# Retention and a gated FFN on one core: four products and six table instructions moved from GpSimd to VectorE, four zero products removed

## The chip, the cores and the metric

The kernel runs on one NeuronCore of a Trainium2 chip. A core has five engines, each with its own instruction queue in program order: TensorE (PE; its weight loads are listed as PEld) multiplies matrices, VectorE (DVE) and ScalarE (ACT) work on tiles, GpSimd (POOL) works on tiles and also issues transfers, and SyncE (SP) issues transfers. Sixteen DMA engines move the data. The metric is the device time of one execution in microseconds (us). Lower is better.

## The reference

For every batch and head a 64 x 64 state runs over 768 tokens, and its output feeds a gated FFN:

```python
# q, k, v: (B=4, H=8, S=768, D=64), float32
for t in range(S):
    state = gamma[h] * state + outer(k[:, :, t], v[:, :, t])
    y[:, :, t] = 1 / sqrt(D) * (q[:, :, t] @ state)
x = y.transpose(0, 2, 1, 3).reshape(3072, 512)
out = (sigmoid(x @ w_gate) * (x @ w_val)) @ w_out      # d_ff = 1536
```

with gamma[h] = 1 - 2^(-5-h).

## The kernel before, in words

The recurrence is done in blocks of 128 tokens (C). Within a block, scores k x q are multiplied by a decay table and then with v; between blocks, a state is summed from scaled k and v. A step `i` stands for one token block and two of the four batches (`t, h = divmod(i, 2)`), so there are twelve. All four batches of one token block, 512 rows, make one FFN tile `t`; there are six. The FFN of a tile has twelve column groups of 128 for gate and value (`up`), each followed by a sigmoid on ACT (line 419) and a product on DVE (line 420), and then the product with `w_out` (`down`).

The schedule is by hand: the order of the calls in the program is the order on each engine. There is no planner with costs. Lines 470 to 501 do the first tile's retention (steps 0 and 1) on a path of its own: transposes on PE (`first_transpose`), scores, products with v (`first_y`). `keep_on(n)` (line 461) puts n products of a zero tile on PE between them; nothing reads their results. Lines 510 to 531 are the first tile's gate and value groups. After this, lines 542 to 574 do the first tile's `down` together with step 2, whose k and q are transposed on PE (`transpose`, line 209). From step 3 on k and q are transposed by DMA (`xbar`, line 216, issued on SP), and the table `plan` (line 577) says after which FFN group each retention block comes.

All loads except two come from POOL's queue (`nc.gpsimd.dma_start`): they convert float32 to bf16 on the way. The order on that queue is: the first tile's k, q and v (line 95), weights of gate and value in slices of 256 columns (line 82, slices 0 to 5), `w_out` in four parts (line 89), and k, q and v of the later steps (lines 66, 70, 60). From `load_next(4)` on, a one-element copy on POOL (`hold`, line 539) waits for a transposed tile before further loads are issued. Every load on POOL after the first eight waits on one of eight semaphores, in turn: so an issue waits until the load eight before it has landed.

Three sets of POOL instructions that are no loads stand between these issues ahead of step 2. `first_scaled` (line 369) makes the scaled k of steps 0 and 1, the tiles `ks`, in four products of 128 x 512; `first_state` (line 372) needs them. `later_tables` (line 176) makes `tabsk` in four copies of 128 x 24 and `maskk` in two products of 128 x 512; `scale_k` (line 222, on POOL) and `mask` (line 251, on DVE) read them from step 2 on.

PE's results go to eight PSUM banks in rotation (`bank`, line 200): each new tile waits until the readers of the one eight before it are done.

Of the kernel before, what the change touches and what calls it, by code (L numbers as in the profile page):

```python
# [11 lines left out]
ALU = mybir.AluOpType  # L12
# [3 lines left out]
def kernel(  # L16
# [12 lines left out]
    nc = tc.nc  # L29
    B, H, S, D = q.shape  # L30
    N_TOK, D_MODEL = out.shape
    D_FF = moe_w_gate.shape[1]
    C = 128
    NT = S // C
    NP = H // 2
# [14 lines left out]
    kn, qn, ks, vs, kqT = {}, {}, {}, {}, {}  # L50
# [29 lines left out]
    def load_w(dst, w, s, kk=slice(0, KT)):  # L80
        cols = slice(s * 256, (s + 1) * 256)
        nc.gpsimd.dma_start(out=dst[:, kk, cols], in_=w.rearrange("(kk p) n -> p kk n", p=128)[:, kk, cols])  # L82

    def load_gate_val(s):
        load_w(wg, moe_w_gate, s)
        load_w(wv, moe_w_val, s)
# [17 lines left out]
    def entry(t, j):  # L104
        return t[:, j * H:(j + 1) * H, :]
# [25 lines left out]
    causal = const.tile([128, 128], F32, name="causal")  # L131
    decay = const.tile([128, 2, NP, C], F32, name="decay")
    maskk = const.tile([128, 2, NP, C], F32, name="maskk")
    tabs = const.tile([128, H, NT], F32, name="tabs")
# [20 lines left out]
    def exps_y(p):  # L155
        nc.scalar.activation(taby[:, p], col, AX.Exp, bias=lsc, scale=lgz[:, 0, p:p + 1])
# [19 lines left out]
    def later_tables():  # L176
        src = tabs.rearrange("s (p e) t -> s e t p", e=2)
        dst = tabsk.rearrange("s t j (p e) -> s j e t p", e=2)
        for j in range(2):
            for e in range(2):  # L180
                nc.gpsimd.tensor_copy(dst[:, j, e], src[:, e ^ j])
        for e in range(2):
            nc.gpsimd.tensor_tensor(maskk[:, e], causal.unsqueeze(1).to_broadcast([128, NP, C]),
                                    tabsk[:, 0, e, 0::2].unsqueeze(2).to_broadcast([128, NP, C]), op=ALU.mult)


# [13 lines left out]
    def bank(shape, dt=F32):  # L200
        return pf.tile(shape, dt, tag="ff", name="ff")
# [4 lines left out]
    def new_kqT(i):  # L206
        kqT[i] = at.tile([128, 2, 2, NP, C], BF16, tag="kqT", name="kqT", bufs=2)
# [142 lines left out]
    def first_scores(i, j):  # L350
        scores(i, j)
        for e, st in enumerate((stA, stB)):
            st[i, j] = at.tile([128, NP, C], BF16, tag=f"sf{e}", name=f"sf{e}", bufs=4)
            nc.vector.tensor_tensor(st[i, j], sc[i, j][e], decay[:, e], op=ALU.mult)

    def first_y(i, j, engs):
        if 0 not in xT:
            new_xT(0, 2)
        c = (2 * i + j) * C
        n = 1 if engs[0] is engs[1] else 2  # L360
        os = [bank([128, NP // n, C]) for _ in range(n)]
        for p in range(NP):
            for e, st in enumerate((stA, stB)):
                nc.tensor.matmul(os[p * n // NP][half(e), p % (NP // n), :], vs[i][:, j * H + 2 * p + e, :], st[i, j][:, p, :],
                                 start=(p % (NP // n) == 0), stop=True, skip_group_check=True)
        for g, eng in enumerate(engs):
            eng(xT[0][g][:, :, c:c + C], os[g] if n == 2 else os[0][:, 2 * g:2 * g + 2])

    def first_scaled(i, j, x):
        nc.gpsimd.tensor_tensor(entry(ks[i], j), x, tabs[:, :, 0].unsqueeze(2).to_broadcast([C, H, D]), op=ALU.mult)  # L370

    def first_state(i):
        z = bank([128, 2, NP, D])
# [87 lines left out]
    def keep_on(n):  # L461
        u = bank([128, 512])
        for _ in range(n):
            nc.tensor.matmul(u, zero[:, :128], zero, start=True, stop=True)  # L464
# [4 lines left out]

    new_kqT(0)  # L470
    new_kqT(1)
    keep_on(11)
    exps_y(0)
    first_transpose(0, 0, 0, dve)
    first_transpose(0, 0, 1, act)
# [5 lines left out]
    exps_y(1)  # L481
    first_transpose(1, 0, 0, act)
    exps_y(2)
    keep_on(1)
    first_scores(0, 1)
    first_transpose(1, 0, 1, act)
    keep_on(2)
# [5 lines left out]
    keep_on(2)  # L493
    first_y(0, 0, (act, act))
    first_scores(1, 1)
    keep_on(1)
    first_y(0, 1, (act, act))
    keep_on(2)
    first_y(1, 0, (dve, act))
# [1 line left out]
    first_y(1, 1, (dve, act))  # L501
    nc.scalar.preload_act_table(AX.Sigmoid)
    first_scaled(0, 0, kf)
    first_scaled(0, 1, entry(kn[0], 1))
    load_gate_val(3)
    first_scaled(1, 0, entry(kn[1], 0))
    first_scaled(1, 1, entry(kn[1], 1))
    load_gate_val(4)
    load_gate_val(5)
    for n1s in ((0, 1), (2, 3)):  # L510
        gates = first_parts(wg, n1s, (3 * C,) if n1s[0] == 0 else ())
        for n1, *ps in zip(n1s, gates, first_parts(wv, n1s)):
# [1 line left out]
    last_constants()  # L514
    zero_scores()
    later_tables()
    gates = [up_part(0, wg, (n1,)) for n1 in (4, 5)]
    for n1, gate in zip((4, 5), gates):
# [111 lines left out]
```

## Time and profile before

| | |
|---|---|
| median of 11 runs | 226.13 us (225.66 to 227.27) |
| the profiled execution | 226.52 us, its span 224.8 us |
| PE busy | 217.0 us, 97% of the span |
| DVE / ACT / POOL busy | 123.0 / 70.6 / 106.8 us |
| mean of DMA engines' busy share | 90% or more in the first 20 of 40 slices |
| first FFN product on PE | 14.90 us |
| last FFN product ends, first tile's transposes of step 2 begin | 37.9 us |
| products of zeros on PE | 19, the first at 1.20 us |

Times in the profile count from the start of the span. The span is 1.7 us shorter than the time of its own execution. A group's busy time is the sum of its instructions; where an engine was idle, the profile names what released it. For a load, "to landing" is the time from its issue on the queue until its last byte is there.

### The profile page before, as it was taken

Reading aid. Unit: us, or ns where it says so; the run is one execution under the profiler, and the core shown is the slowest. Engines: PE = TensorE matmul, PEld = TensorE weight load, DVE = VectorE, ACT = ScalarE, POOL = GpSimd, SP = SyncE. Lnnn points to the kernel's source line nnn. Section 1 sums busy time; section 2 is a strip of 40 time slices with the busy share of each in tenths; the row PEclk is TensorE's granted clock in tenths of the full one; section 3 lists DMA queues with packets and bytes.
Section 4 is the critical chain, followed back from the end, with each engine's and each line's share of the span. In section 5 each row is a group of like instructions: output and inputs, shape, how many; then the busy total and the mean of one; then the engine's idle time right before and its main releaser. Section 6 shows DMA issues by size and latency. Waiting matters only on the chain.

```text
span 224.8 us, 6389 instructions
## 1 busy us (share of the span) xinstructions
PE 217.0 (97%) x2765; PEld 127.1 (57%) x2770; DVE 123.0 (55%) x242; ACT 70.6 (31%) x122; POOL 106.8 (48%) x130
## 2 busy tenths in 40 slices
PE   7899998999999998999999999999999999999994
PEld 2554443459999665556556556555555555555554
DVE  6753873085894784945925754934654922333301
ACT  4883332334233211332321433321433321333221
POOL 8999997886983945909467082460000000000000
PEclk9999999999999999999999999999999999999999
DMA  9999999999999999999979979999600012100022
GB/s 130 145 173 189 160 178 168 184 152 270 133 151 131 120 139 195 157 106 61 139 107 194 163 50 114 79 137 143 140 3 0 3 47 96 47 4 0 4 93 93
DMA packets 105820, 25.84 MB, mean 115 GB/s; under 512 B 94784, under 2 KB 102848, under 8 KB 105792
## 3 DMA queue, kind: packets, MB, share of 16 engines
q0 software_dynamic: 80960, 13.90, 85.9%
q1 hardware_dynamic: 23648, 11.21, 24.1%
q8 instruction: 21, 0.34, 0.7%
q10 hardware_dynamic: 1184, 0.33, 0.6%
q14 instruction: 7, 0.06, 0.1%
HBM read 28.31 MB, written 6.29 MB: 154 GB/s over the span
## 4 chain that ended last, share of the span: by engine, by line
PE 60%; DMA 20%; POOL 18%; issue 1%; DVE 0%; POOLq 0%; SPq 0%
PE ff L391 56%; DMA kqX<-qn 7%; DMA qn<-in_q_dram 4%; DMA wo<-in_moe_w_out_dram 3%; DMA kn<-in_k_dram 3%; POOL wv L82 2%; POOL wg L82 2%; POOL ks L370 2%; DMA kqX<-kn 2%; PE ff L278 2%; POOL kn L70 2%; POOL vs L95 2%; POOL kn L66 1%; POOL kn L95 1%; POOL qn L95 1%
## 5 line engine op out<-in xcount | busy, mean ns | idle before, releaser
L420 DVE TENSOR_TENSOR hT<-gs,ff 128x512 bf16<-128x512 f32 x72 | 48.4, 686 | 51.9 <-PE ff L391 46.4
L391 PE MATMUL ff<-xT,wg 128*64 128x512 bf16 (+2 forms) x607 | 70.0, 346 | 0.1
L391 PE MATMUL ff<-xT,wv 128*64 128x512 bf16 (+2 forms) x608 | 70.0, 345 | 0.0
L419 ACT ACTIVATE gs<-ff 128x512 f32<-128x512 f32 x72 | 42.8, 597 | 82.9 <-PE ff L391 80.3
L391 PE MATMUL ff<-wo,hT 128*64 128x512 bf16 (+3 forms) x580 | 64.6, 361 | 0.1
L391 PEld LDWEIGHTS <-wv 128*64 128x64 bf16 (+1 forms) x608 | 35.4, 109 | 23.4
L391 PEld LDWEIGHTS <-hT 128*64 128x64 bf16 (+1 forms) x582 | 32.7, 109 | 27.1
L391 PEld LDWEIGHTS <-wg 128*64 128x64 bf16 (+1 forms) x608 | 34.9, 109 | 23.2 <-DVE xT L294 0.2
L261 DVE TENSOR_TENSOR st<-ff,maskk 128x256 bf16<-128x256 f32 (+2 forms) x76 | 35.1, 492 | 9.0 <-PE ff L248 8.0
L441 ACT COPY ob<-ff 128x512 f32<-128x512 f32 x23 | 13.5, 586 | 57.6 <-PE ff L391 57.5
L294 DVE TENSOR_TENSOR xT<-ff,taby 128x512 bf16<-128x512 f32 x20 | 12.9, 686 | 24.3 <-PE ff L278 24.3
L540 POOL COPY held<-kqX 128x1 bf16<-128x1 bf16 x7 | 1.3, 185 | 36.0 <-DMA kqX<-qn 33.8
L224 POOL TENSOR_TENSOR ks<-kn,tabsk 128x1024 bf16<-128x1024 bf16 x8 | 15.6, 1947 | 1.6 <-DMA kn<-in_k_dram 1.6
L70 POOL DMA_DIRECT2D qn<-in_q_dram x20 | 15.5, 803 | 0.0
L70 POOL DMA_DIRECT2D kn<-in_k_dram x20 | 15.2, 774 | 0.0
L60 POOL DMA_DIRECT2D vs<-in_v_dram x10 | 12.1, 1212 | 1.1 <-DMA wo<-in_moe_w_out_dram 0.9
L66 POOL DMA_DIRECT2D kn<-in_k_dram x10 | 9.3, 928 | 1.8 <-issue 1.7
L314 DVE TENSOR_TENSOR zb<-za,tabz 128x512 bf16<-128x512 f32 x10 | 9.4, 943 | 0.0
L66 POOL DMA_DIRECT2D qn<-in_q_dram x10 | 9.3, 925 | 0.0
L464 PE MATMUL ff<-zero 128*128 128x512 bf16 x19 | 7.6, 527 | 1.2 <-DVE zero L139 1.2
L278 PE MATMUL ff<-st,vs 128*64 128x128 bf16 x160 | 6.4, 222 | 0.0
L82 POOL DMA_DIRECT2D wg<-in_moe_w_gate_dram x8 | 6.4, 822 | 0.0
(74 smaller groups left out, 117.3 us busy)
## 6 DMA issues: line engine op xcount, KB each, us to landing
out_dram<-ob SPq DMA_DIRECT2D x23, 256.0 KB, 2.8
vs<-in_v_dram POOLq DMA_DIRECT2D x10, 256.0 KB, 7.4
kn<-in_k_dram POOLq DMA_DIRECT2D x13, 128.0 KB, 4.9
qn<-in_q_dram POOLq DMA_DIRECT2D x13, 128.0 KB, 4.9
wo<-in_moe_w_out_dram POOLq DMA_DIRECT2D x4, 384.0 KB, 7.1
kn<-in_k_dram POOLq DMA_DIRECT2D x20, 64.0 KB, 3.8
qn<-in_q_dram POOLq DMA_DIRECT2D x20, 64.0 KB, 4.5
wg<-in_moe_w_gate_dram POOLq DMA_DIRECT2D x4, 256.0 KB, 5.2
```

The lines of the kernel that those rows point to most:

```text
L60: nc.gpsimd.dma_start(out=vs[i], in_=v[2 * h:2 * h + 2, :, t * C:(t + 1) * C, :].rearrange("b h s d -> s (b h) d"))
L66: nc.gpsimd.dma_start(out=tiles[i][:, 0:H], in_=src[0])
L70: nc.gpsimd.dma_start(out=dst[:, e], in_=pairs[:, 1 - e])
L82: nc.gpsimd.dma_start(out=dst[:, kk, cols], in_=w.rearrange("(kk p) n -> p kk n", p=128)[:, kk, cols])
L224: nc.gpsimd.tensor_tensor(ks[i], kn[i], tabsk[:, i // 2].rearrange("s j h -> s (j h)").unsqueeze(2) .to_broadcast([C, 2 * H, D]), op=ALU.mult)
L261: nc.vector.tensor_tensor(st[i, j][to, :, n], sc[i, j][e][of, :, n], maskk[to, e ^ j, :, n], op=ALU.mult)
L278: nc.tensor.matmul(y[i, j][half(e), p, :], vs[i][:, j * H + 2 * p + e, :], st[:, p, :], start=False, stop=True, skip_group_check=True)
L294: nc.vector.tensor_tensor(xT[t][0][:, :, c:c + C], y[i, j], taby, op=ALU.mult)
L391: nc.tensor.matmul(o[c], w[:, c], x, **marks)
L419: nc.scalar.activation(g, ps[0], AX.Sigmoid)
L420: nc.vector.tensor_tensor(hT[t][:, n1s[0]:n1s[-1] + 1, lo:hi], g.rearrange("p (i n) -> p i n", n=n), ps[1].rearrange("p (i n) -> p i n", n ...
L441: nc.scalar.copy(ob, o)
```

## The change

The four products of `first_scaled` and the six instructions of `later_tables` go from POOL's queue to DVE's; their operands, results and place among the calls stay. On POOL the three loads of weight slices 3, 4 and 5 then follow one another. Of `keep_on`'s products, two of the first eleven go, and two single ones later.

```diff
@@ later_tables
         for j in range(2):
             for e in range(2):
-                nc.gpsimd.tensor_copy(dst[:, j, e], src[:, e ^ j])
+                nc.vector.tensor_copy(dst[:, j, e], src[:, e ^ j])
         for e in range(2):
-            nc.gpsimd.tensor_tensor(maskk[:, e], causal.unsqueeze(1).to_broadcast([128, NP, C]),
+            nc.vector.tensor_tensor(maskk[:, e], causal.unsqueeze(1).to_broadcast([128, NP, C]),
                                     tabsk[:, 0, e, 0::2].unsqueeze(2).to_broadcast([128, NP, C]), op=ALU.mult)
@@ first_scaled
     def first_scaled(i, j, x):
-        nc.gpsimd.tensor_tensor(entry(ks[i], j), x, tabs[:, :, 0].unsqueeze(2).to_broadcast([C, H, D]), op=ALU.mult)
+        nc.vector.tensor_tensor(entry(ks[i], j), x, tabs[:, :, 0].unsqueeze(2).to_broadcast([C, H, D]), op=ALU.mult)
@@ the order of the first tile
     new_kqT(0)
     new_kqT(1)
-    keep_on(11)
+    keep_on(9)
     exps_y(0)
...
     exps_y(2)
-    keep_on(1)
     first_scores(0, 1)
...
     first_scores(1, 1)
-    keep_on(1)
     first_y(0, 1, (act, act))
...
     first_scaled(0, 0, kf)
     first_scaled(0, 1, entry(kn[0], 1))
-    load_gate_val(3)
     first_scaled(1, 0, entry(kn[1], 0))
     first_scaled(1, 1, entry(kn[1], 1))
-    load_gate_val(4)
-    load_gate_val(5)
+    for n in range(3, 6):
+        load_gate_val(n)
```

## The prediction

> **What bounds the kernel now.** I read the page first, then PE's waits by stretch, then the timelines of PE, POOL and DVE, and last the rate of the transfers in quarter microseconds.
>
> The page's first part says that PE is nearly always busy, so only its 7.8 us of idle time can be won, or busy time that is not needed.
>
> ```profile
> PE 217.0 (97%) x2765; PEld 127.1 (57%) x2770; DVE 123.0 (55%) x242; ACT 70.6 (31%) x122; POOL 106.8 (48%) x130
> ```
>
> The list of waits, for PE alone (us in total, times, longest), asked for 0 to 26, 26 to 60 and 60 to 225 us, names what it waited for. Of these the reader is to see one wait in each stretch: weights ahead of the first FFN groups, q of step 2, and one transposed tile.
>
> ```profile
> PE ff L409 <- DMA wv<-in_moe_w_val_dram: 0.3, 1, 0.3
> ...
> PE ff L213 <- DMA qn<-in_q_dram: 1.4, 1, 1.4
> ...
> PE ff L248 <- DMA kqX<-qn: 0.6, 1, 0.6
> ```
>
> PE's timeline places the second one: k's four transposes are over at 38.29, q's start at 39.64. From 17.09 to 38.29 and again to 86.07 PE runs without a gap of note, and from 86.67 to the end too.
>
> ```profile
> 37.90 0.39 PE L213 MATMUL ff<-ident,kn 128*128 128x128 bf16 x4
> 39.64 0.40 PE L213 MATMUL ff<-ident,qn 128*128 128x128 bf16 x4 [1.36 <-DMA qn<-in_q_dram]
> ```
>
> So the end is set by PE's work plus two late transfers, 1.36 and 0.60 us. Both are loads that stand behind POOL's own work (start, duration, in us):
>
> ```profile
> 17.39 1.21 POOL L370 TENSOR_TENSOR ks<-kf,tabs 128x512 bf16<-128x512 f32 x1
> 18.42 1.20 POOL L370 TENSOR_TENSOR ks<-kn,tabs 128x512 bf16<-128x512 bf16 x1
> ...
> 20.98 2.15 POOL L370 TENSOR_TENSOR ks<-kn,tabs 128x512 bf16<-128x512 bf16 x2
> 23.00 0.83 POOL L82 DMA_DIRECT2D wg<-in_moe_w_gate_dram  x1
> ...
> 26.00 0.74 POOL L181 COPY tabsk<-tabs 128x24 f32<-128x24 f32 x4
> 26.68 2.06 POOL L183 TENSOR_TENSOR maskk<-causal,tabsk 128x512 f32<-128x512 f32 x2
> 28.66 1.57 POOL L89 DMA_DIRECT2D wo<-in_moe_w_out_dram  x2
> ```
>
> But a load that is issued sooner lands sooner only if the DMA engines had nothing to do. The DMA view of 20 to 30 us gives their rate in 40 slices of 0.25 us:
>
> ```profile
> GB/s 195 201 199 195 191 168 164 203 190 197 195 178 176 184 190 193 191 96 86 72 90 154 162 184 188 195 186 190 184 180 168 92 82 84 137 172 201 193 191 258
> ```
>
> It is full, near 190, but for two dips: at 24.25 to 25.75 and at 27.75 to 28.75.
>
> **The change, part by part.** *POOL, ten instructions less.* Start to start, the first pair of products holds POOL from 17.39 to 19.41, the second from 20.98 to 23.00, the tables from 26.00 to 28.66: 2.02 + 2.02 + 2.66 = 6.70 us by which POOL could be ahead when it comes to w_out (22.0 instead of 28.66) and to k and q of step 2. That is an upper end which the transfers don't grant: an issue waits for the landing of the load eight before it, and these land at the DMA rate. What is won at q's landing is the two dips. First: (94 + 104 + 118 + 100 + 36 + 28) / 190 x 0.25 = 0.63 us. Second: (98 + 108 + 106 + 53) / 190 x 0.25 = 0.48 us. The first follows from POOL: slice 4 of gate was issued only at 23.00, behind the products. The second is not clear: slice 5 of gate had been issued at 24.53, so there should have been descriptors; it coincides with the mask products on POOL. I count it half: gain 0.63 + 0.24, about 0.9 us, ends 0.6 and 1.1. With 0.9, q lands at about 38.7 and 0.45 of PE's 1.36 us remains. Nothing is lost before: slices 0 to 2, on which the first groups wait, are issued before 17.39 in both kernels, and they land in the order of their issue.
>
> What is late next? The second wait, 0.60 us at 86.67, hangs on a chain of transfers that starts with k of step 3 (landed 47.94), then transposed tile, hold, loads 4 and 5, transposed tile, hold, load 6, transposed tile. k of step 3 comes in the same full stream behind q of step 2, so this chain moves by the same 0.9 us as PE does. The wait stays at 0.6. Past it PE has no wait in the trace.
>
> *DVE, ten instructions more.* The rows between which they go, and the row of a neighbour:
>
> ```profile
> 14.81 0.42 DVE L367 CAST xT<-ff 128x256 bf16<-128x256 f32 x1 [0.24 <-PE ff L364]
> ...
> 18.45 1.28 DVE L420 TENSOR_TENSOR hT<-gs,ff 128x512 bf16<-128x512 f32 x2 [3.21 <-PE ff L409]
> ...
> 27.59 2.31 DVE L314 TENSOR_TENSOR zb<-za,tabz 128x512 bf16<-128x512 f32 x2
> ```
>
> The four products take the price of DVE's two decay products of 128 x 512 from SBUF at 3.08 (1.29 for two): 4 x 0.65 = 2.6 us, from 15.23 to 17.8. They lie in the 3.21 us before 18.45, with 0.6 to spare. At 690 ns each it is 2.8, still inside; they'd have to cost 0.8 each to delay a product of the FFN, and even that only matters if a PSUM bank comes free late, eight tiles on. The two mask products are 1.3 us, the four copies of 24 columns about 0.1 each (six small ones of DVE took 0.45 at 6.88): 1.7 us, which start at 24.55 where DVE had 0.37 us idle. So the product at 24.92 moves to about 26.3, the state copies from 26.39 to 27.7, the casts behind them to 29.0. Who waits? The banks of values 4 and 5 are wanted at 29.70 and 30.56, those of the two states at 31.42 and 32.29, and are free by 27.7 and 29.0: at least 2 us of cover. If that cover were gone the cost would be 1.3 us, once.
>
> *Here a rule speaks for and against.* By the row, DVE's two casts at 27.59 took 2.31 us while POOL ran its mask products, against a median of 686 ns for one. The Trainium skill, SBUF — State Buffer, Who interferes with whom, says that a DVE instruction with two SBUF inputs and a GpSimd instruction that reads SBUF lock each other out. This case agrees, and the casts give back 0.9 us of the 1.7. The same section says that DVE's copies can take, in a mode of two ports, the ports through which POOL writes the descriptors of its loads. By the rule the four small copies, 0.4 us, would stop an issue for as long; POOL then waits for landings anyway, so I take zero. The products, by the same page, hold only the read side.
>
> *Four zero products less.* Warm ones cost 0.22 us of PE each (0.866 for four FFN products), the first eleven 0.425 (4.88 less 0.634, over 10). Taken off: 2 x 0.425 + 2 x 0.22 = 1.3 us of PE work. All of it lies before 14.90, where PE waits for loads anyway (v at 11.92, 12.91, 13.79 and 14.46, weights at 14.90, 15.53, 16.86 and 17.09), so the gain is zero. The price can be the clock. The row: eleven zero products took 634 ns each, all later ones 379, and four transposes took 0.63 us at 5.86 and 0.40 at 6.33; so the clock rose near 6.3. The skill, TensorE: Matmul & The Clock Gate, Part 1, says that it rises after a busy window of about 3.4 us, whose place is free. Nine products end at 1.20 + 9 x 0.425 = 5.0; k's transposes start as they do now, near 5.5. By the row the 0.4 us gap does nothing. By the rule, a run of 3.8 us holds a whole window in few phases only, and the clock may rise one window later, at 9.7: the five groups of transposes (0.23 each), two of scores (0.25) and a zero product there, 1.9 us, double, of which 1.5 us idle time in those 3.4 takes most. That leaves 0 to 0.5 us ahead of the FFN. I take 0.
>
> **The sum.** Span 224.8 - 0.9 = 223.9; with the 1.7 around it 225.6 for an execution like the profiled one. That one was 0.39 above the median of the runs (226.52 against 226.13); so 226.13 - 0.9 = **225.2 us**.
>
> **The rivals.** *Both waits go.* If the stream gains more than the dips show, PE is rid of 1.36 and the chain behind it of 0.60: 1.96 us, 224.2. For it speaks POOL's 6.7 us, and that the chain of work gives POOL 18% of the span; against it the full rate around the dips. *The first wait only moves.* PE gains 0.6 to 0.9 at 39.64, but the later chain does not move along (its third transposed tile took 11.9 us to land, among other loads), and PE gives it back at 86.67: 226.1, no change. For it: that chain is long and runs through three holds; against it: no engine in it but POOL and SP. *The clock is still half as the FFN starts* (slower). PE's gaps are longer with fewer zeros and the rise slips past 14.9. Each us of half clock in dense products costs 0.5; it decides from 1.8 us on, where 0.9 is eaten. A whole window, 3.4 us, costs 1.7: 226.9; two, 228.6. Against it: at half clock PE's work there doubles, which closes the gaps and so brings the rise.
>
> **How the numbers follow.** Main case 0.57; both waits go 0.12; no change 0.16; clock 0.15. What a measurement of this kernel can tell from no change is about 0.3%, 0.68 us: below 225.45 is faster, above 226.81 slower. Of the main case (224.9 to 225.6) four fifths are below 225.45: 0.46, with the second case 0.58 faster. The other fifth and the no-change case, with a part of the clock's, make 0.29 within, and 0.13 slower. The range 224.3 to 226.9 leaves out the far ends of the second and last case.
>
> **What would show it.** PE's wait for q of step 2 falls to 0.2 to 0.7 us; the dip at 24.25 is gone and, if it was POOL's, the one at 27.75; w_out's first issue comes at 22 to 24 us, with POOL waiting for landings; DVE's ks products end by 18.0 at 0.65 each; its casts take 0.69 each. Transposes from 6.3 on take 0.40 for four. The prediction is wrong if zero products or FFN products after 9.7 us take 634 ns, if the wait for the transposed tile grows by what the first lost, or if PE waits for DVE between 25 and 33 us.

## The result, and the profile after

The changed kernel takes 224.58 us (median of 12 runs, 223.95 to 225.58) against 226.01 us (47 runs, 225.5 to 227.4). The ratio is 0.9935, 95% interval 0.9919 to 0.9951: 0.65% faster; the medians are 1.43 us apart. The forecast was 225.2. Its profiled execution took 225.58 us, the slowest of the twelve, with a span of 223.8 against 224.8.

PE is 1.3 us less busy (the zero products), POOL 6.6 us:

```profile
PE 215.7 (96%) x2760; PEld 126.4 (56%) x2766; DVE 124.3 (56%) x252; ACT 70.6 (32%) x122; POOL 100.2 (45%) x120
```

PE's waits from 26 us on, in the same view as before (us in total, times, longest): that for q of step 2 is gone, and that for the transposed tile of step 6 is, in this execution, twice as long.

```profile
PE ff L248 <- DMA kqX<-qn: 1.2, 1, 1.2
```

PE's timeline shows both places. The transposes of q follow those of k at once (38.22 instead of 39.64); those of k do not come sooner (38.00 instead of 37.90), so nothing was won ahead of them. The scores of step 6 start at 85.80 instead of 86.67 (first the changed kernel, then the last two rows of the kernel before):

```profile
38.00 0.39 PE L213 MATMUL ff<-ident,kn 128*128 128x128 bf16 x4
38.22 0.39 PE L213 MATMUL ff<-ident,qn 128*128 128x128 bf16 x4
...
84.22 0.42 PE L271 MATMUL ff<-kqX,zb 64*64 64x128 bf16 x16
85.80 0.55 PE L248 MATMUL ff<-kqX 64*64 64x128 bf16 x32 [1.16 <-DMA kqX<-qn]
...
85.65 0.42 PE L271 MATMUL ff<-kqX,zb 64*64 64x128 bf16 x16
86.67 0.59 PE L248 MATMUL ff<-kqX 64*64 64x128 bf16 x32 [0.60 <-DMA kqX<-qn]
```

POOL's queue (start, duration, idle before and who ended it) now goes from weight slice to weight slice, and is at w_out at 21.87 instead of 28.66. From there on it waits for landings, time and again; so whenever it waits, loads issued earlier are still under way:

```profile
20.31 0.94 POOL L82 DMA_DIRECT2D wg<-in_moe_w_gate_dram  x1
21.07 0.93 POOL L82 DMA_DIRECT2D wv<-in_moe_w_val_dram  x1
21.87 0.87 POOL L89 DMA_DIRECT2D wo<-in_moe_w_out_dram  x1
23.19 0.77 POOL L89 DMA_DIRECT2D wo<-in_moe_w_out_dram  x1 [0.46 <-DMA wv<-in_moe_w_val_dram]
24.58 0.91 POOL L66 DMA_DIRECT2D kn<-in_k_dram  x1 [0.62 <-DMA wg<-in_moe_w_gate_dram]
```

The first of q's three loads for step 2 is issued at 28.80 instead of 32.62. From issue to landing it took, in the kernel before and in the changed one:

```profile
DMA to landing us min/median/max: 7.0/7.0/7.0
...
DMA to landing us min/median/max: 8.9/8.9/8.9
```

So it landed at 39.6 before and lands at 37.7 now: 1.9 us sooner, and ahead of PE, which comes to it at 38.2.

The rate of the transfers from 20 to 30 us, in slices of 0.25 us, has neither dip, and the mean is 197 GB/s instead of 169:

```profile
GB/s 199 186 180 184 184 197 195 197 197 197 199 193 193 199 197 197 199 197 193 197 195 197 197 195 199 219 191 195 186 199 195 197 195 195 197 195 203 195 203 262
DMA packets 3882, 1.97 MB, mean 197 GB/s; under 512 B 123, under 2 KB 3880, under 8 KB 3880
```

DVE's timeline has the ten instructions in it: the k products in the gap before 18.55, the tables from 24.65, the FFN product behind them at 26.22 instead of 24.92, and the two casts in 1.28 us instead of 2.31:

```profile
15.16 0.68 DVE L370 TENSOR_TENSOR ks<-kf,tabs 128x512 bf16<-128x512 f32 x1
15.76 1.89 DVE L370 TENSOR_TENSOR ks<-kn,tabs 128x512 bf16<-128x512 bf16 x3
...
24.65 0.82 DVE L181 COPY tabsk<-tabs 128x24 f32<-128x24 f32 x4
25.01 1.28 DVE L183 TENSOR_TENSOR maskk<-causal,tabsk 128x512 f32<-128x512 f32 x2
26.22 1.28 DVE L420 TENSOR_TENSOR hT<-gs,ff 128x512 bf16<-128x512 f32 x2
...
28.61 1.28 DVE L314 TENSOR_TENSOR zb<-za,tabz 128x512 bf16<-128x512 f32 x2
```

### The profile page after: what moved, and what is told of

Its sections match the earlier page's. It is cut to its first block, busy times and chain, and to the rows that moved or that the text cites. A ratio compares the mean times of both kernels' runs of the same rounds, so it can differ in the third digit from the quotient of the medians.

```text
span 223.8 us, 6376 instructions
## 1 busy us (share of the span) xinstructions
PE 215.7 (96%) x2760; PEld 126.4 (56%) x2766; DVE 124.3 (56%) x252; ACT 70.6 (32%) x122; POOL 100.2 (45%) x120
## 4 chain that ended last, share of the span: by engine, by line
PE 60%; DMA 25%; POOL 12%; issue 1%; DVE 0%; POOLq 0%; SPq 0%
PE ff L391 56%; DMA kqX<-qn 6%; DMA wo<-in_moe_w_out_dram 5%; DMA qn<-in_q_dram 5%; DMA kn<-in_k_dram 3%; DMA wv<-in_moe_w_val_dram 3%; DMA kqX<-kn 2%; PE ff L278 2%; POOL kn L70 2%; POOL vs L95 2%; POOL wg L82 2%; POOL wv L82 1%; POOL kn L95 1%; POOL kn L66 1%; POOL qn L95 1%; PE ff L248 1%
## 5 line engine op out<-in xcount | busy, mean ns | idle before, releaser
L314 DVE TENSOR_TENSOR zb<-za,tabz 128x512 bf16<-128x512 f32 x10 | 7.0, 704 | 0.0
L464 PE MATMUL ff<-zero 128*128 128x512 bf16 x14 | 5.6, 542 | 1.2 <-DVE zero L139 1.2
L82 POOL DMA_DIRECT2D wv<-in_moe_w_val_dram x8 | 6.7, 872 | 0.0
```

## The experiments

The theory after the result: GpSimd's own products let the stream of loads run thin; without them it stays full, q of step 2 is there in time, and nothing else in the change counts. The rivals: the removed zero products carry part of the gain; the tables do; moving work to VectorE counts as such; or it is GpSimd's computing, wherever it stands, that slows the transfers.

**The zero products alone.**

```diff
# the kernel before, with
-    keep_on(11)
+    keep_on(9)
...
-    keep_on(1)
     first_scores(0, 1)
...
-    keep_on(1)
     first_y(0, 1, (act, act))
```

> The kernel before with only the four zero products taken out. If the gain comes from the load stream alone: within 0.3 us of the kernel before (226.0), PE's wait for q of step 2 stays near 1.4 us and both dips in the load rate stay. If the removed PE work of 1.3 us counts, or PE's start into the FFN does: 0.4 us or more faster. If fewer zeros let the clock rise late: slower, with products of 634 ns after 9.7 us.

Measured: 226.28 us, ratio 1.0014 (0.9997 to 1.0031). 1.3 us of PE work less is worth nothing. Both waits and both dips are there, as in the kernel before:

```profile
PE ff L213 <- DMA qn<-in_q_dram: 1.0, 1, 1.0
PE ff L248 <- DMA kqX<-qn: 0.4, 1, 0.4
```

Since loads and work are those of the kernel before, this profile (226.03 us) also says what an execution near the old median looks like: 0.98 and 0.42 us of waiting, not the 1.36 and 0.60 of the execution profiled first (226.52).

**The k products alone.**

```diff
# the kernel before, with
-        nc.gpsimd.tensor_tensor(entry(ks[i], j), x, ...)
+        nc.vector.tensor_tensor(entry(ks[i], j), x, ...)
# and the loads of weight slices 3, 4 and 5 after all four of them, as in the change
```

> The kernel before with the four k products on VectorE and the weight loads 3 to 5 in a row; the tables stay on GpSimd, all zero products stay. If only GpSimd's late issue of weight slice 4 empties the stream: both dips gone (the tables then stand ahead of w_out, whose turn at the DMA engines comes only near 29.7 us), wait for q near zero, 224.6 to 225.0. If the mask products on GpSimd slow the stream while they run: one dip of about 0.5 us stays near 24 to 26 us, and about 225.0 to 225.4.

Measured: 224.66 us, ratio 0.9943 (0.9916 to 0.997). Both dips are gone and PE waits for nothing from 26 us on. POOL still makes the mask products, from 23.98 on (it even waits 1.23 us for VectorE's `causal`), and the rate while they run stays near 195:

```profile
GB/s 182 182 174 186 166 164 174 188 184 197 195 193 199 197 199 197 188 193 199 201 199 193 195 195 193 201 231 180 195 188 193 193 201 201 191 197 197 191 191 268
```

The slices of 164 to 188 GB/s ahead of 22.5 us do not make q late; its transposes follow those of k at once:

```profile
38.40 0.39 PE L213 MATMUL ff<-ident,kn 128*128 128x128 bf16 x4
38.63 0.39 PE L213 MATMUL ff<-ident,qn 128*128 128x128 bf16 x4
```

So the second dip was not due to the mask products, as I had half assumed.

**The tables alone.**

```diff
# the kernel before, with
-                nc.gpsimd.tensor_copy(dst[:, j, e], src[:, e ^ j])
+                nc.vector.tensor_copy(dst[:, j, e], src[:, e ^ j])
...
-            nc.gpsimd.tensor_tensor(maskk[:, e], ...)
+            nc.vector.tensor_tensor(maskk[:, e], ...)
```

> The kernel before with only the tables on VectorE; k products on GpSimd, all zero products stay. The first dip (24.25 to 25.75 us) stays in any case. If the second dip was due to the mask products on GpSimd it is gone, q lands 0.5 us sooner, and the time is about 225.5. If it follows from the first one, by whatever way, it stays and the time is 226.0 within 0.3.

Measured: 225.81 us, ratio 0.9988 (0.9968 to 1.0009), no change that can be told. Both dips stay, the second though w_out is issued at 26.08, 2.6 us sooner:

```profile
GB/s 186 193 197 199 193 178 168 170 152 176 182 168 162 170 164 188 176 117 117 90 104 199 160 168 180 191 178 166 193 197 190 150 115 137 111 160 180 178 164 170
```

In this profile PE waits 0.7 us for q, against 1.4 in the kernel before and 1.0 with the zero products alone, and not at all for the transposed tile of step 6. The profiled execution (225.24 us) was the fastest of its 22.

```profile
PE ff L213 <- DMA qn<-in_q_dram: 0.7, 1, 0.7
```

**The change with its zero products put back.**

```diff
# the changed kernel, with
-    keep_on(9)
+    keep_on(11)
# and keep_on(1) again ahead of first_scores(0, 1) and of first_y(0, 1, ...)
```

> The changed kernel with the four zero products put back. If the zero products are worth nothing: 224.6, the same as the changed kernel. If they carried part of its gain: 225.0 or more.

Measured: 224.64 us, ratio 0.9949 (0.9925 to 0.9973). That is the changed kernel's time; with the first experiment, the zero products are settled from both sides.

**Far fewer zero products.**

```diff
# the changed kernel, with
-    keep_on(9)
+    keep_on(4)
```

> The changed kernel with 4 first zero products instead of 9: PE is busy only to 3.3 us and idle until 5.4. If the clock only has to be up when the FFN starts: products take longer up to some 10 to 13 us, the FFN starts at most 0.5 us later, time 224.6 to 225.1. If the clock is still half at 15 us: FFN products of over 600 ns for up to 3.4 us, and 225.5 to 226.3 or more.

Measured: 224.83 us, ratio 0.9943 (0.9914 to 0.9973), 0.25 us more than the changed kernel had at first and 0.46 more than beside it (last experiment); the intervals overlap. Here the clock does come late. In PE's timeline four transposes take over 0.6 us and two zero products 1.06 until 11.2 us, and the normal 0.40 only from 12.12; the FFN starts at 15.45 instead of 15.13:

```profile
9.91 0.61 PE L347 MATMUL ff<-ident,qn 128*128 128x128 bf16 x4
10.31 1.06 PE L464 MATMUL ff<-zero 128*128 128x512 bf16 x2
11.16 0.63 PE L347 MATMUL ff<-ident,kn 128*128 128x128 bf16 x4
...
12.12 0.40 PE L347 MATMUL ff<-ident,qn 128*128 128x128 bf16 x4
...
15.45 0.82 PE L409 MATMUL ff<-xT,wg 128*128 128x384 bf16 x4
```

So a clock that rises some 5.5 us later costs 0.3 us at the start of the FFN. The reason is in PE's waits: ahead of the FFN the changed kernel waits 1.2 us for k, q and v, and this one for no load, so the slower products filled time in which PE would have waited for loads. Whether the clock rose by a window of 3.4 us, as the expectation takes from the prediction, these two profiles do not show.

**The k products left on GpSimd, but later.**

```diff
# the kernel before, with the tables on VectorE and
-    first_scaled(0, 0, kf)
-    first_scaled(0, 1, entry(kn[0], 1))
     load_gate_val(3)
+    load_gate_val(4)
+    first_scaled(0, 0, kf)
+    first_scaled(0, 1, entry(kn[0], 1))
     first_scaled(1, 0, entry(kn[1], 0))
     first_scaled(1, 1, entry(kn[1], 1))
-    load_gate_val(4)
     load_gate_val(5)
```

> The kernel before with the tables on VectorE, and the four k products left on GpSimd but behind the loads of weight slices 3 and 4 instead of among them; all zero products stay. If the place of the products among the loads is what counts, not the engine: no dip, no wait for q, 224.6, like the changed kernel. If GpSimd's work slows the transfers while it runs, wherever it stands: a dip of 0.5 us or more, 225.2 or more.

Measured: 224.55 us, ratio 0.9933 (0.9903 to 0.9964): the whole gain, with all four products on GpSimd. They run from 20.42 to 24.46, between slices 4 and 5:

```profile
20.42 1.18 POOL L370 TENSOR_TENSOR ks<-kf,tabs 128x512 bf16<-128x512 f32 x1
21.44 3.18 POOL L370 TENSOR_TENSOR ks<-kn,tabs 128x512 bf16<-128x512 bf16 x3
24.46 0.84 POOL L82 DMA_DIRECT2D wg<-in_moe_w_gate_dram  x1
```

While they run the rate is near 197 (first line, 20 to 30 us), so computing on GpSimd as such does not slow the transfers. A dip comes all the same, at 28 to 31 us (second line, 27 to 37 us), but it leaves q in time: PE has no wait from 26 us on.

```profile
GB/s 193 197 199 197 197 193 197 197 195 195 195 199 199 197 195 195 193 203 195 199 191 195 197 201 199 217 172 188 190 197 193 184 154 148 162 170 170 164 170 90
...
GB/s 190 197 193 184 154 148 162 170 170 164 170 90 102 125 154 135 147 180 201 209 201 193 193 205 205 205 210 212 180 173 175 157 156 152 154 153 151 153 153 153
```

So "no dip" was wrong, and "the place counts, not the engine" right in the time.

**Half of the products on GpSimd.** Two kernels, with one pair on each engine, and the order of calls, tables and zero products of the kernel before.

```diff
# the kernel before, with the pair i on GpSimd, the other on VectorE
-        nc.gpsimd.tensor_tensor(entry(ks[i], j), x, ...)
+        (nc.gpsimd if i == 0 else nc.vector).tensor_tensor(entry(ks[i], j), x, ...)   # i == 1 in the second kernel
```

> The kernel before with only the second pair of k products (step 1) on VectorE; the first pair stays on GpSimd ahead of weight slice 3, tables and all zero products as before. If what counts is GpSimd's lead over the DMA engines: slice 4 is then issued at about 21.0 us, 3 us ahead of its turn near 24.3, so there is no dip, and 224.6, the whole gain from half of the move. If each product on GpSimd costs its share: a dip stays, and about 225.3.

> The kernel before with only the first pair of k products (step 0) on VectorE; the second pair stays on GpSimd between slices 3 and 4. By the lead: slice 4 again issued at about 21.0 us, no dip, 224.6. If the place between slices 3 and 4 is what hurts: the dip at 24 to 26 us stays, and 225.3 or more.

Measured: the first pair left on GpSimd, 225.09 us, ratio 0.9948 (0.9929 to 0.9968); the second pair left, 224.44, ratio 0.9937 (0.9914 to 0.9961). In both, PE's wait for q is zero. The rates from 20 to 30 us, the kernel with the first pair on GpSimd ahead, then the one with the second:

```profile
GB/s 186 182 174 195 195 197 193 195 182 193 191 186 176 139 162 160 168 172 156 117 135 143 162 182 184 197 164 182 158 193 199 199 199 219 184 193 197 193 199 195
...
GB/s 176 182 188 199 199 193 193 197 199 197 197 193 199 197 195 195 184 186 197 197 195 197 197 195 199 217 193 193 195 193 197 199 193 195 193 203 188 197 262 186
```

With the first pair a shallow dip is left at 23.25 to 25.75, though slice 4 is issued at 21.19; with the second there is none, though it stands where the deeper dip of the kernel before seemed to come from. So the second kernel came out as the lead had it (its turn near 24.3 us was set too early, though: in the kernel before, slice 3's second load lands at 25.6). The first did not: the dip stayed, and its time is near the 225.3 of the other expectation, though the two kernels' intervals overlap. Its profile has no wait for q that could account for the 0.65 us between their medians; the FFN ends 0.7 us later than in the second (38.59 against 37.86), most of it lost to waits for gate weights before 16.5 us, where the two programs issue the same loads. Whether that is more than one execution's is not shown.

**The second wait, and the changed kernel again.**

```diff
# the changed kernel, with the scores of step 6 one FFN group later
-        (12, hold, 6), (12, load_next, 7), (14, block, 4, 5, 5), (18, block, 5, 6, 6)],
+        (12, hold, 6), (12, load_next, 7), (14, block, 4, 5, 5), (18, block, 5, None), (19, block, None, 6, 6)],
```

> The changed kernel with the scores, masks and state of step 6 one FFN group later (after group 19 of tile 1 instead of 18, with step 5's output still after group 18). If the wait for the transposed tile of step 6, 0 to 1.2 us in the profiles so far, is what is left of PE's idle time after 26 us: the wait is gone, the median 0.3 to 0.6 us below the changed kernel's (about 224.2) and the slowest runs fall most. If that wait is covered or comes back elsewhere: no change against the changed kernel, 224.6.

> The changed kernel once more, beside the three others on the same chip: 224.6 within 0.3; its wait for the transposed tile of step 6 may differ from the 1.2 us of its first profile, between 0 and 1.2.

Measured: with the later scores 224.49 us, ratio 0.9929 (0.9902 to 0.9956); the changed kernel beside it 224.37 us, ratio 0.9924 (0.99 to 0.9948). There is nothing left to win there: the changed kernel's second profile (224.19 us, span 222.4) has no wait at all after 26 us. Its scores of step 6 start at 84.41:

```profile
84.17 0.42 PE L271 MATMUL ff<-kqX,zb 64*64 64x128 bf16 x16
84.41 0.52 PE L248 MATMUL ff<-kqX 64*64 64x128 bf16 x32
```

The later scores make neither the median nor the slowest run (225.99 against 225.44) better. The 1.16 us of the first profile was that execution's. No kernel tried here is faster than the changed one by more than can be told.

## Why the prediction was right, and where not

The direction, the place and the cause were right: the time went from PE's wait for q of step 2, because GpSimd's k products no longer held up the loads. The size was too small: 0.9 us forecast, 1.4 measured. By its mechanism the result is less the main case, in which 0.45 us of the first wait and all of the second stay, than the rival that both waits go: in the changed kernel's second profile both are gone. The measured gain lies below that rival's 1.96 us because the rival, too, was worked out on an execution that waited longer than most ("The base", below).

**The term of the sum that was mis-sized** is q's landing: 0.9 us sooner in the sum, 1.9 in the profiles. The dips between 20 and 30 us were not all that could be won. The rate over that stretch rose from 169 to 197 GB/s, which is 10 x (1 - 169 / 197) = 1.4 us of a full stream, against 1.11 for the two dips whole: the plateau near 190 between them, which I took for full, was not. And the kernel before went on losing behind 30 us. Landings in the two profiles, in us:

| load | before | after |
|---|---|---|
| value weights, slice 3 | 25.6 | 25.6 |
| value weights, slice 4 | 29.0 | 28.5 |
| value weights, slice 5 | 32.6 | 31.2 |
| w_out, second part | 36.9 | 35.0 |
| q of step 2, first load | 39.6 | 37.7 |

The 1.9 us are more than the 1.36 of the wait, so none of it remained.

**The second dip** I laid half on the mask products. The runs with the tables alone moved (dip stays) and the k products alone moved (dip gone) show that it too hangs on the k products.

**"The wait stays at 0.6"**, the chain of transposed tiles moving with PE, was wrong as a rule. The wait was 1.16 us in one profile of the changed kernel and nothing in the other. It was nothing in five more kernels: the k products alone, the zero products put back, the k products later, and the two halves. With four first zeros it was 0.21. But it was also nothing with the tables alone, where q was late. PE came to it 1.43 us sooner (84.64 against 86.07, the ends of the products before it), the tile 0.87 us sooner in the first profile and at least 2.26 in the second (84.41 against 86.67). So the chain's gain varies by execution, and how much of it is due to the change is open.

**The base.** I set 0.9 us off against the median of the runs, but worked it out on a profile whose two waits, 1.96 us together, were longer than the 1.40 of another execution with the same loads (zero products alone, 226.03 us) and the 0.66 of the one with the tables alone (225.24 us). Take these two waits off the span of each profile, and the twelve spans come to 222.4 to 223.0 us, whatever the kernel. So what sets the kernels apart is these waits, to within 0.6 us, and taking away the 1.40 of an execution near the median gives what was measured.

**DVE's side** went as worked out. The k products cost 2.57 us and end at 17.65 (forecast 17.8), the product behind the tables starts at 26.22 (26.3), the casts take 0.69 each, as forecast, or 1.28 for the two, since one begins before the other has ended. In the same way the four small copies hold up the next product by only 0.36 us (from 24.65 to 25.01; 0.4 forecast), though their row spans 0.82. The wait of those casts for GpSimd, for which the prediction names the Trainium skill (SBUF — State Buffer, Who interferes with whom), is gone. It goes also where GpSimd keeps the mask products but has ended them before the casts begin: 1.28 us in the kernel with the k products alone (masks to 26.0, casts from 28.09) and in both halves. So the overlap made it, as that page has it. No wait of PE for DVE appears after 15 us. For the port rule on descriptors the runs show nothing: the changed kernel's issues before 22 us lasted 0.87 to 0.94 us with DVE at work or idle, and in the kernel with the k products alone 0.75 to 0.78 with the same work on DVE.

**The zero products** were priced at nothing, and the two kernels that take them out and put them back show it. The clock rival fell: in the changed kernel transposes take 0.40 for four from 6.18 us on. The run with four first zeros shows that the clock can come late; up to 12 us that costs 0.3 us at the FFN's start, inside the 0 to 0.5 that I had put on one window.

## What to carry to other kernels

An engine that both computes and issues loads must stay ahead of the transfers: look at how long before the landing of the load ahead of it each load is issued, not at the engine's busy share or its share of the chain. Here 6.6 us less work on GpSimd was worth 1.4 us, and so, within the noise, was leaving the same four products on GpSimd behind two more weight slices (with the tables moved, which alone were worth nothing). To size such a gain, follow the landings up to the load that is waited for, not the rate in one stretch, and cap the gain by that wait, over more than one execution.

## What the runs showed of the hardware that was not expected

A pause in GpSimd's issues can make loads late although loads issued before it are still under way. In the full stream of the changed kernel a load of 256 columns lands 1.3 us behind the one ahead of it. For the first load behind each pause, the profiles give:

| first load behind the pause | issued so long before the load ahead of it landed, us | landed behind that load by, us |
|---|---|---|
| slice 4: the kernel before, zero products alone, tables alone | 2.6, 2.5, 2.8 | 2.1, 1.5, 2.1 |
| slice 3: the same three | 3.5, 3.4, 3.3 | 1.3, 1.3, 1.5 |
| slice 5: k products later | 3.8 | 1.4 |
| slice 3: first pair on GpSimd | 3.9 | 1.3 |
| slice 4: second pair on GpSimd | 4.5 | 1.3 |

So a lead of some 3 us is wanted here, which is an estimate from these nine cases.

That does not explain all of it. A dip can also come one or more loads behind the pause. After the four products between slices 4 and 5 the issues went on at 24.46, and the rate fell at 28 to 31 us. After the first pair alone they went on at 19.65, and the rate fell at 23.25 to 25.75. The second pair alone, of the same length, left no dip. What the DMA engines lack in those dips is not shown by any run; it stays open.

A product of 128 x 512 (bf16 input) took 1.15 us on GpSimd and 0.69 on VectorE; three in a row took 3.18 (k products later) and 1.89 us.
